# Pooled values of batch 1 on GpSimd, shared casts of q, a later memset and an earlier turn of q in an attention and MoE kernel

## The chip, the cores and the metric

The kernel runs on one core of a Trainium2 chip. The metric is the device time of one execution in microseconds, and the time of the kernel before is the median of three runs.

## The reference

The first stage is an attention whose keys and values are means over groups of eight positions. The second stage is a two-layer network over the attention's output, with g = h - tanh(h) between the layers.

```python
batch, heads, S, D, pool = 8, 8, 576, 64, 8
k_p = k.reshape(B, H, S // pool, pool, D).mean(axis=3)
v_p = v.reshape(B, H, S // pool, pool, D).mean(axis=3)
attn = softmax(q @ k_p.T / sqrt(D))          # 576 x 72 for each head
x = (attn @ v_p).transpose(0, 2, 1, 3).reshape(4608, 512)
h = x @ w_in                                 # 512 x 2048
out = (h - tanh(h)) @ w_out                  # 2048 x 512
```

Inputs and output are float32.

## The kernel before

The kernel takes the 4608 tokens in nine groups of 512 (`NG`). Groups 0 to 7 are the first 512 rows of each batch, and group 8 gathers the last 64 rows of all batches (`xT_last`). TensorE (PE) works through the matmuls in an order written out by hand, and each of the other engines has its own written order too. Nothing is moved by a scheduler: `tc.manual_schedule()` keeps the program's order on each engine, and semaphores between engines follow from the data.

For a batch the work is this. Keys and values come in as float32 (`k_raw`, `v_raw`, two buffers each, so batches 1, 3, 5 share one). `pool_k` adds the eight rows of a group in three steps, four, two and one at a time, and leaves `kd`, two copies of the pooled keys in bf16. PE or the DMA transposes these, and the pieces are put into `KB`. The values are added up in the same way and spread into `VB`, which also carries a column of the constant 8. Queries are cast to bf16 into `q_bf`, turned into `qT` (by `q_pe_transpose` for batches 0 and 1, and by `q_dma_transpose` on the SP queue from batch 2 on). Then follow scores, `exp` on ScalarE into `E`, the product with `VB`, and a division by the last column on VectorE (`x_sb`). The result is transposed into `xT`.

Group 0 of the network uses plain matmuls: `mlp_h_mms` with `mlp_h_act` for the first layer, `mlp_o(g, tb, qd, gts)` for one quarter `qd` of the second layer's sum of the block `tb` of 128 tokens (four matmuls of 512 columns). Between those quarters the attention of batch 1 is interleaved; this is the first stage that the change touches. From group 1 on the second layer is a Strassen-like scheme with seven products (`products`) in place of eight, for which sums and differences of quarters of w_out are prepared (`sum0` to `sum3`, `negated`, in `w2s`). In these groups `h_pair` computes two of the 16 blocks of the first layer into two banks, takes tanh on ScalarE (L647) and the difference on VectorE (L648). The seven pairs of group 1 use the banks 6, 4, 2, 6, 0, 2, 4 in turn. The queries of batch 2 are cast (`q_cast_part`, L196 and L201, ScalarE) and turned (`q_dma_transpose`, L214 and L219, SP) between these pairs; this is the second stage that the change touches. The scores of the next batch (`head_scores`, L446) stand between the halves of the products and use the banks 2 and 3, then 4 and 5.

In the stage of batch 1 the queries come from `q1_bf` and `q1_tail`, which lie in the space of `w2s` until the sums are written there. Two copies at L1017 reorder them into `q_bf`, four heads each, one by VectorE and one by ScalarE. `evac` takes a PSUM tile out to SBUF, by the engine named. PSUM tiles of this stage come in turn from the banks 4, 5, 6, 7: one for the keys, one for their remainder, four for q, one for its tail, then the scores. `pool_v1(ta, tb)` adds the values of batch 1 for the tiles `ta` to `tb` on VectorE (L303) and places them with `v_main` (L323) or, for the remainder, `v_left` (L333). The instruction that it returns is stored as `placed`, and two of GpSimd's `sum3` instructions are made to wait for it.

GpSimd (POOL) builds constants at the start, issues the loads of the weights (`load_w1`, `load_w2`), pools the keys of batch 1 up to the last addition, which VectorE does (L270), issues two more loads of w_out, and pools keys and values of the later batches.

Of the kernel before, what the change touches and what calls it, by code (L numbers as in the profile page):

```python
# [34 lines left out]
NM = 4  # L35
# [8 lines left out]
def kernel(  # L44
# [178 lines left out]
    def q_pe_transpose(b, hps, eng=None):  # L223
        qT, _ = q_tiles(b)
        for hp in hps:
            ps = ps_any([128, QA], FP32, "qT_ps")
            for j in range(R):
                nc.tensor.matmul(
                    ps[:, j * 128 : (j + 1) * 128],
                    lhsT=q_bf[:, j, 2 * hp : 2 * hp + 2, :].rearrange("p h d -> p (h d)"),  # L230
                    rhs=ident[:, :],
                    start=True,
                    stop=True,
                )
            evac(qT[:, :, hp, :], ps.rearrange("p (j c) -> p j c", j=R), eng)
# [61 lines left out]
                out=vps[b][:, :, :], in0=r[:, :, 0, :], in1=r[:, :, 1, :], op=ALU.add  # L297
            )

    def pool_v1(ta, tb):  # L300
        r = v_raw[1].rearrange("p t (j d) -> p t j d", d=D)
        for n in (4, 2, 1):
            nc.vector.tensor_tensor(  # L303
                out=r[:, ta:tb, 0:n, :],
                in0=r[:, ta:tb, 0:n, :],
                in1=r[:, ta:tb, n : 2 * n, :],
                op=ALU.add,
            )
        if ta == NM:
            return v_left(VB[1], r[:, NM, 0:1, :], nc.vector)  # L310
        return v_main(VB[1], r[:, :, 0:1, :], nc.vector, ta, tb)

    vps = {}

# [6 lines left out]
    def v_main(vb, vs, eng, t0, t1):  # L321
        n = t1 - t0
        return eng.tensor_tensor(  # L323
            out=vb[:, 2 * t0 : 2 * t1, 0:D].rearrange("p (t s) d -> p t s d", s=2),
            in0=vs[:, t0:t1, :, :].to_broadcast([128, n, 2, D]),
            in1=mask[:, 2 * t0 : 2 * t1, :]
            .rearrange("p (t s) o -> p t s o", s=2)
            .to_broadcast([128, n, 2, D]),
            op=ALU.mult,
        )  # L330

    def v_left(vb, vs, eng):
        return eng.tensor_tensor(  # L333
            out=vb[:, 2 * NM :, 0:D],
            in0=vs.to_broadcast([128, NM, D]),
            in1=mask[:, 2 * NM :, :].to_broadcast([128, NM, D]),
            op=ALU.mult,
        )
# [21 lines left out]
    def k_transpose(b, alloc, engs=(nc.vector.tensor_copy, nc.scalar.copy)):  # L360
        kd = kdups.pop(b)
        ps = alloc([128, NM, 128], FP32, "kT_ps")
        for t in range(NM):
            turn_tile(ps[:, t, :], kd, t)
        kb_main(KB[b % 2], ps, 0, NM, engs)
        ps = alloc([128, 128], FP32, "kT_ps")
        turn_tile(ps[:, :], kd, NM)
        kb_left(KB[b % 2], ps, nc.vector.tensor_copy)
# [37 lines left out]
    def scores_wide(b, ts):  # L406
        if b not in E_tiles:
            E_tiles[b] = work.tile([128, H, S], BF16, name="E", tag="E", bufs=1)[:, 0:NT, :]
        E = E_tiles[b]
        for t in ts:  # L410
            ps = ps_any([128, QA], FP32, "s_ps")
            score_mms(b, t, ps[:, :], False)
            nc.scalar.activation(out=E[:, t, 0:QA], in_=ps[:, :], func=ACT.Exp, scale=SCALE)
# [196 lines left out]
    def mlp_o(g, tb, qd, gts):  # L610
        if qd == 0:
            o_tiles[tb] = bank((1, 2, 3, 0)[tb], [128, DM])
        o_ps = o_tiles[tb]
        i0 = W2_ORDER[qd]
        for i in range(i0, i0 + 4):
            nc.tensor.matmul(  # L616
                o_ps[:, :],
                lhsT=gts[i][:, tb * 128 : (tb + 1) * 128],
                rhs=w2b[:, i, :],
                start=(i == 0),  # L620
                stop=(i == NHID - 1),
            )
        if qd == 3:
            if tb < 2:
                nc.vector.tensor_copy(out=O[:, tb, :], in_=o_ps[:, :])
            else:
                nc.scalar.copy(out=O[:, tb, :], in_=o_ps[:, :])
            if tb % 2:
                store(g, tb - 1, tb + 1, nc.sync)
# [136 lines left out]
    def load_w2(i, n):  # L766
        w2_dmas.append(
            nc.gpsimd.dma_start(out=w2b[:, i : i + n, :], in_=w2_src[:, i : i + n, :])
        )
# [39 lines left out]

    make_identity(nc, ident)  # L810
    nc.gpsimd.memset(q_bf[64:128, R, :, :], 0.0)
    nc.gpsimd.memset(w2s[64:128, 3, 6:8, :], 0.0)
    nc.gpsimd.memset(mask[:, :, :], 1.0)
    for m, base, step, cm in (
        (mask[:, 0 : 2 * NM : 2, 0], G - 1, 0, -1),
# [27 lines left out]
        out=q1_bf, in_=q[1, :, 0:QA, :].rearrange("h (p j) d -> p h j d", j=R)  # L843
    )
    load_w2(8, 4)
    nc.gpsimd.memset(k_raw[1][:, NM, :], 0.0)
    nc.gpsimd.memset(v_raw[0][:, NM, :], 0.0)
    nc.gpsimd.memset(KB[1][:, :], 0.0)
# [164 lines left out]
    pool_k(1, nc.gpsimd, last=nc.vector)  # L1013
    load_w2(4, 4)
    load_w2(12, 4)
    for h, copy in ((0, nc.vector.tensor_copy), (4, nc.scalar.copy)):
        copy(  # L1017
            out=q_bf[:, 0:R, h : h + 4, :].rearrange("p j h d -> p h j d"),
            in_=q1_bf[:, h : h + 4, :, :],
        )  # L1020
    mlp_o(0, 0, 0, gts)
    mlp_o(0, 1, 0, gts)
    mlp_o(0, 2, 0, gts)
    k_transpose(1, ps_any, (nc.vector.tensor_copy, nc.vector.tensor_copy))
    mlp_o(0, 3, 0, gts)
    q_pe_transpose(1, (0, 1), "act")
    sum1(0)
    pool_v1(0, 2)
    q_pe_transpose(1, (2, 3), "act")
    q_pe_tail(1)  # L1030
    scores_wide(1, (0,))
    placed = pool_v1(2, 4)
    mlp_o(0, 0, 1, gts)
    scores_wide(1, (1,))
    mlp_o(0, 1, 1, gts)
    scores_wide(1, (2, 3))
    scores_ends(1)
    negated(0)
    sum2(0)
# [23 lines left out]
    turn1(3)  # L1063
    av(1, 4, ps_any, True)
    sum0(4)
    for tb in range(4):
        mlp_o(0, tb, 3, gts)
    x_pairs.pop((1, 0))
    x_pairs.pop((1, 1))
    x_dma_transpose(1, 2)  # L1070
    pool_k(2, nc.gpsimd)
    k_dma_transpose(2)
    load_k(3)
    pool_v(2, nc.gpsimd, (0, 1))
    k_place(2, nc.gpsimd.tensor_copy)
# [2 lines left out]
    for g in range(1, NG):  # L1078
        nb = g + 1 if g + 1 < B else None
        nn = g + 2 if g + 2 < B else None  # L1080
        for p in range(NP - 1):
            if g == 1 and 3 <= p < 6:
                q_cast_part(2, p - 3)
                q_dma_transpose(2, p - 3)
            if nb is not None and g > 1 and p < 3:
                q_cast_part(nb, p)
            h_pair(g, p, ((6, 4, 2, 6, 0, 2, 4) if g == 1 else (0, 2, 4, 6, 0, 2, 4))[p], p % 2)
            if g == 1 and p == 1:
                sum2(4)
            if g == 1 and p == 2:  # L1090
                w_sum(b12, b22, b12, ALU.subtract)
            if g == 1 and p == 5:
                load_v(3)
                load_q(3)
                v_spread(2, nc.gpsimd)
            if 3 <= p < 6:
                sum_p(2 * p - 6, 2 * p - 4)
            if g > 1 and p == 0:
                if nb is not None:
                    k_dma_transpose(nb)  # L1100
                store(g - 1, 2, 4, nc.gpsimd)
                store(g - 1, 0, 2, nc.gpsimd)
                if nb is not None:
                    k_place(nb, nc.gpsimd.tensor_copy)
            if nb is not None and g > 1 and p < 3:
                q_dma_transpose(nb, p)
            if nb is not None and g > 1 and p == 2:
                v_spread(nb)
                if nn is not None:
                    load_k(nn)  # L1110
                    load_v(nn)
                    load_q(nn)
        h_one(g, NP - 1, 1, 0, 2)
        h_one(g, NP - 1, 0, 1, 3)
        sum_p(6, 8)
        sum_q(0, 4)
        sum_q(4, 8)
        if nb is not None:
            sum_d(0, 2)
            sum_d(2, 4)  # L1120
        ps_a = Banks(2, 3, 4, 5, 0, 1)
        for u in range(14):
            n, half = u // 2, u % 2
            bk, lhs, rhs = products[n]
            if n == 6 and g == NG - 1:
                break
            product(g, bk, lhs, rhs, 4 * half, 4 * half + 4, n < 2)
            if half:
                after_product(g, n)
            if nb is not None:  # L1130
                if u == 0:
                    head_scores(nb, (0, 1))
                if u == 2:
                    head_scores(nb, (2, 3), True)
                if u in (5, 6, 7, 8, 10):
                    blk = (5, 6, 7, 8, 10).index(u)
                    av(nb, blk, ps_b1, True)
                    if blk in (1, 3, 4):
                        x_dma_transpose(nb, blk // 2)
                if u == 6 and nn is not None:  # L1140
                    pool_k(nn, nc.gpsimd)
                    pool_v(nn, nc.gpsimd)
        if g < NG - 1:
            nc.scalar.copy(out=O[:, 0:2, 0:HD], in_=chain(g, C1))  # L1144
# [37 lines left out]
```

## Time and profile before

| what | value |
|---|---|
| time, median of three runs | 286.15 us (286.08 to 286.72) |
| profiled execution, its own time | 286.49 us |
| profiled execution, span from first to last instruction | 284.7 us |
| granted TensorE clock | 0.997 |
| PE busy | 275.9 us (97% of the span) |
| VectorE (DVE) busy | 224.2 us (79%) |
| ScalarE (ACT) busy | 155.5 us (55%) |
| GpSimd (POOL) busy | 119.1 us (42%) |
| moved by DMA | 49.82 MB, 175 GB/s on average |

The span is that of the profiled execution, and what lies around it is not in the trace. Busy time of an engine is the time in which an instruction of it is under way; an instruction that waits for something inside the engine counts as busy. Start times in the views are microseconds from the start of the span. In the timeline a row is a start, a length, the engine, the line of the kernel, the operation, what is written and read, the number of instructions merged in it, and, in brackets, the engine's idle time before it with what ended it.

### The profile page before, as it was taken

To read this page: it belongs to the slowest core of one execution; us is meant where nothing else is said; L and a number is where in the kernel's file an instruction comes from. 1 tells how busy PE (TensorE), PEld (TensorE's weight loads), DVE (VectorE), ACT (ScalarE), POOL (GpSimd) and SP (SyncE) were. 2 spreads that over 40 slices of the span, in tenths; PEclk is the share of its full clock that TensorE was granted. 3 is DMA by queue.
4 is the path that set the end of the run, shared out by engine and by line. 5 is a ranking of instruction groups with operands and counts; after the bars stand their busy time and mean duration, and the time that the engine had idled before them with its cause. 6 is when DMAs were issued, how large, how long until landed. Compare 5 with 4: busy or idle time off the path is not lost.

```text
span 284.7 us, 5459 instructions
## 1 busy us (share of the span) xinstructions
PE 275.9 (97%) x2156; PEld 180.2 (63%) x2156; DVE 224.2 (79%) x339; ACT 155.5 (55%) x208; POOL 119.1 (42%) x129
## 2 busy tenths in 40 slices
PE   7899999998999999999999999999999999999994
PEld 2454455644894489448954895479547954884583
DVE  5569898789875998599859985998599839936983
ACT  2837676386628672857186718670868056216610
POOL 8810809972299019901990099009910110010000
PEclk9999999999999999999999999999999999999998
DMA  7999999889847894769789986896640540012014
GB/s 245 230 210 279 259 206 305 270 236 229 246 83 144 290 324 83 143 226 350 130 107 270 324 149 124 272 323 131 114 161 0 76 157 0 2 74 77 0 39 111
DMA packets 66731, 49.82 MB, mean 175 GB/s; under 512 B 42088, under 2 KB 55928, under 8 KB 66706
## 3 DMA queue, kind: packets, MB, share of 16 engines
q1 hardware_dynamic: 56082, 34.92, 48.8%
q0 software_dynamic: 8432, 12.72, 18.8%
q10 hardware_dynamic: 2192, 1.84, 2.2%
q8 instruction: 17, 0.28, 0.5%
q14 instruction: 8, 0.07, 0.1%
HBM read 36.70 MB, written 9.44 MB: 162 GB/s over the span
## 4 chain that ended last, share of the span: by engine, by line
PE 90%; DMA 4%; ACT 2%; issue 1%; DVE 1%; ACTq 0%
PE PS L634 36%; PE PS L691 35%; PE PS L588 5%; PE PS L616 5%; PE PS L472 3%; PE PS L446 3%; DMA qT<-q_bf 2%; DMA q_raw<-in_q_dram 2%; PE PS L398 1%; PE PS L781 1%; PE PS L487 1%; ACT q_bf L196 1%; ACT qT L144 1%; PE PS L875 0%; PE PS L936 0%
## 5 line engine op out<-in xcount | busy, mean ns | idle before, releaser
L634 PE MATMUL PS<-xT,w1b 128*128 128x512 bf16 (+1 forms) x504 | 98.0, 355 | 0.0
L648 DVE TENSOR_TENSOR Gt<-PS,TS 128x1024 bf16<-128x1024 f32 x56 | 68.4, 1222 | 33.7 <-ACT TS L647 33.7
L634 PEld LDWEIGHTS <-w1b 128*128 128x128 f16 x576 | 56.3, 98 | 52.8
L647 ACT ACTIVATE TS<-PS 128x1024 f32<-128x1024 f32 x56 | 57.4, 1025 | 29.5 <-PE PS L634 27.4
L735 POOL TENSOR_TENSOR m<-O,m 128x512 f32<-128x512 f32 x6 | 7.6, 1259 | 77.3 <-ACT m L733 77.3
L691 PE MATMUL PS<-w2s,Dg 128*128 128x256 f16 x256 | 30.2, 273 | 0.0
L467 ACT ACTIVATE E<-PS 72x1024 bf16<-72x1024 f32 (+1 forms) x30 | 26.1, 930 | 4.8 <-PE PS L446 4.6
L691 PEld LDWEIGHTS <-Gt 128*128 128x128 bf16 x256 | 23.6, 98 | 6.9 <-issue 2.5
L261 POOL TENSOR_TENSOR k_raw<-k_raw 128x512 f32<-128x512 f32 (+2 forms) x13 | 21.1, 1636 | 14.6 <-DMA k_raw<-in_k_dram 14.6
L691 PEld LDWEIGHTS <-P 128*128 128x128 bf16 x256 | 24.6, 98 | 3.0
L691 PEld LDWEIGHTS <-Dg 128*128 128x128 bf16 x256 | 24.6, 98 | 2.8
L656 DVE TENSOR_TENSOR P<-Gt 128x1024 bf16<-128x1024 bf16 x32 | 22.0, 687 | 0.5
L707 POOL DMA_DIRECT2D out_dram<-O x14 | 7.7, 551 | 31.7 <-DVE O L745 29.5
L742 ACT COPY m<-PS 128x512 f32<-128x512 f32 x8 | 4.7, 586 | 29.6 <-PE PS L691 29.6
L666 DVE TENSOR_TENSOR Dg<-Gt 128x1024 bf16<-128x1024 bf16 x32 | 20.4, 683 | 0.0
L523 DVE TENSOR_TENSOR x_sb<-PS,rden 128x512 bf16<-128x512 f32 x28 | 19.4, 692 | 1.0
L282 POOL TENSOR_TENSOR v_raw<-v_raw 128x512 f32<-128x512 f32 (+1 forms) x12 | 18.2, 1537 | 0.0
L691 PE MATMUL PS<-w2s,Gt 128*128 128x256 f16 x128 | 16.4, 273 | 0.0
L691 PE MATMUL PS<-w2b,P 128*128 128x256 f16 x128 | 16.3, 273 | 0.0
L691 PE MATMUL PS<-w2s,Q 128*128 128x256 f16 x128 | 16.3, 272 | 0.0
L691 PE MATMUL PS<-w2b,Gt 128*128 128x256 f16 x128 | 16.3, 272 | 0.0
L1144 ACT COPY O<-PS 128x512 f32<-128x512 f32 x7 | 4.1, 587 | 21.9 <-PE PS L691 21.9
(125 smaller groups left out, 403.9 us busy)
## 6 DMA issues: line engine op xcount, KB each, us to landing
k_raw<-in_k_dram SPq DMA_DIRECT2D x7, 1024.0 KB, 5.9
out_dram<-O POOLq DMA_DIRECT2D x14, 512.0 KB, 4.3
v_raw<-in_v_dram SPq DMA_DIRECT2D x6, 1024.0 KB, 8.0
q_raw<-in_q_dram SPq DMA_DIRECT2D x6, 1024.0 KB, 10.6
w1b<-in_moe_w_in_dram POOLq DMA_DIRECT2D x4, 512.0 KB, 13.3
w2b<-in_moe_w_out_dram POOLq DMA_DIRECT2D x4, 512.0 KB, 16.6
v_raw<-in_v_dram SPq DMA_DIRECT2D x2, 512.0 KB, 12.5
out_dram<-O SPq DMA_DIRECT2D x2, 512.0 KB, 3.5
```

The costliest lines, as they stand in the source:

```text
L261: eng.tensor_tensor(out=r[:, ta:tb, 0:4, :], in0=r[:, ta:tb, 0:4, :], in1=r[:, ta:tb, 4:8, :], op=ALU.add,)
L282: eng.tensor_tensor(out=r[:, ta:tb, 0:4, :], in0=r[:, ta:tb, 0:4, :], in1=r[:, ta:tb, 4:8, :], op=ALU.add,)
L467: nc.scalar.activation(out=e, in_=ps, func=ACT.Exp, scale=SCALE)
L523: nc.vector.tensor_tensor(out=x_sb[:, :, :, :], in0=ps[:, :, :, 0:D], in1=rden[:, :, :, :].to_broadcast([128, 2, 4, D]), op=ALU.mult,)
L588: nc.tensor.matmul(h_tiles[i][:, :], lhsT=w1b[:, fb, i * 128 : (i + 1) * 128], rhs=xT[g][:, :, fb, :], start=(fb == 0), stop=(fb == NFB - 1),)
L616: nc.tensor.matmul(o_ps[:, :], lhsT=gts[i][:, tb * 128 : (tb + 1) * 128], rhs=w2b[:, i, :], start=(i == 0), stop=(i == NHID - 1),)
L634: nc.tensor.matmul(dst[:, t0 * 128 : t1 * 128], lhsT=w1b[:, fb, i * 128 : (i + 1) * 128], rhs=x[:, t0:t1, fb, :], start=(fb == 0), stop=(f ...
L647: nc.scalar.activation(out=t2, in_=PS[:, b0 : b0 + 2, :], func=ACT.Tanh)
L648: nc.vector.tensor_sub(out=Gt[:, p, :, :], in0=PS[:, b0 : b0 + 2, :], in1=t2)
L656: nc.vector.tensor_tensor(out=P[:, a:b, :], in0=Gt[:, a:b, 0, :], in1=Gt[:, a:b, 1, :], op=ALU.add)
L666: return nc.vector.tensor_tensor(out=Dg[:, a:b, :, :], in0=Gt[:, a:b, :, 0:HT], in1=Gt[:, a:b, :, HT:TG], op=ALU.subtract,)
L691: nc.tensor.matmul(part(g, bk, tt), lhsT=lhs(k, slice(tt * 128, (tt + 1) * 128)), rhs=rhs[:, k, :], start=(first and k == 0 and (tt == 0 o ...
```

## The change

Six edits are in it.

- The three additions for the main tiles of batch 1's values are made by GpSimd, for all four tiles at once, right behind its two last loads of w_out. VectorE places the result in two instructions, later than before. The remainder (`ta == NM`) stays on VectorE.
- Both copies of batch 1's q into `q_bf` are made by VectorE.
- The four PSUM tiles of q of batch 1 are taken out by ScalarE and VectorE in turn, and two of them are turned ahead of the last quarter-0 output block. `sum1(0)` stands behind them, and the four scores stand in twos.
- A memset of part of `w2s` on GpSimd moves behind the first loads.
- The last quarter of group 0's output, with its stores, is written behind the transposes of `x_end` and of batch 2's `kd`, which changes the order on SP.
- The casts and transposes of q of batch 2 begin at pair 2 instead of pair 3 of group 1; the loads of v and q of batch 3 and the spread of batch 2's values follow at pair 4 instead of 5.

```diff
--- before.py
+++ after.py
@@ -297,18 +297,18 @@
                 out=vps[b][:, :, :], in0=r[:, :, 0, :], in1=r[:, :, 1, :], op=ALU.add
             )
 
-    def pool_v1(ta, tb):
+    def pool_v1(ta, tb, eng=nc.vector):
         r = v_raw[1].rearrange("p t (j d) -> p t j d", d=D)
         for n in (4, 2, 1):
-            nc.vector.tensor_tensor(
+            eng.tensor_tensor(
                 out=r[:, ta:tb, 0:n, :],
                 in0=r[:, ta:tb, 0:n, :],
                 in1=r[:, ta:tb, n : 2 * n, :],
                 op=ALU.add,
             )
         if ta == NM:
-            return v_left(VB[1], r[:, NM, 0:1, :], nc.vector)
-        return v_main(VB[1], r[:, :, 0:1, :], nc.vector, ta, tb)
+            v_left(VB[1], r[:, NM, 0:1, :], nc.vector)
+        return r[:, :, 0:1, :]
 
     vps = {}
 
@@ -809,7 +809,6 @@
 
     make_identity(nc, ident)
     nc.gpsimd.memset(q_bf[64:128, R, :, :], 0.0)
-    nc.gpsimd.memset(w2s[64:128, 3, 6:8, :], 0.0)
     nc.gpsimd.memset(mask[:, :, :], 1.0)
     for m, base, step, cm in (
         (mask[:, 0 : 2 * NM : 2, 0], G - 1, 0, -1),
@@ -843,6 +842,7 @@
         out=q1_bf, in_=q[1, :, 0:QA, :].rearrange("h (p j) d -> p h j d", j=R)
     )
     load_w2(8, 4)
+    nc.gpsimd.memset(w2s[64:128, 3, 6:8, :], 0.0)
     nc.gpsimd.memset(k_raw[1][:, NM, :], 0.0)
     nc.gpsimd.memset(v_raw[0][:, NM, :], 0.0)
     nc.gpsimd.memset(KB[1][:, :], 0.0)
@@ -1013,27 +1013,29 @@
     pool_k(1, nc.gpsimd, last=nc.vector)
     load_w2(4, 4)
     load_w2(12, 4)
-    for h, copy in ((0, nc.vector.tensor_copy), (4, nc.scalar.copy)):
-        copy(
+    for h in (0, 4):
+        nc.vector.tensor_copy(
             out=q_bf[:, 0:R, h : h + 4, :].rearrange("p j h d -> p h j d"),
             in_=q1_bf[:, h : h + 4, :, :],
         )
+    vs = pool_v1(0, NM, nc.gpsimd)
     mlp_o(0, 0, 0, gts)
     mlp_o(0, 1, 0, gts)
     mlp_o(0, 2, 0, gts)
     k_transpose(1, ps_any, (nc.vector.tensor_copy, nc.vector.tensor_copy))
+    q_pe_transpose(1, (0,), "act")
+    q_pe_transpose(1, (1,), "dve")
     mlp_o(0, 3, 0, gts)
-    q_pe_transpose(1, (0, 1), "act")
+    q_pe_transpose(1, (2,), "act")
+    q_pe_transpose(1, (3,), "dve")
+    q_pe_tail(1)
+    v_main(VB[1], vs, nc.vector, 0, 2)
+    placed = v_main(VB[1], vs, nc.vector, 2, 4)
     sum1(0)
-    pool_v1(0, 2)
-    q_pe_transpose(1, (2, 3), "act")
-    q_pe_tail(1)
-    scores_wide(1, (0,))
-    placed = pool_v1(2, 4)
+    scores_wide(1, (0, 1))
     mlp_o(0, 0, 1, gts)
-    scores_wide(1, (1,))
+    scores_wide(1, (2, 3))
     mlp_o(0, 1, 1, gts)
-    scores_wide(1, (2, 3))
     scores_ends(1)
     negated(0)
     sum2(0)
@@ -1063,13 +1065,13 @@
     turn1(3)
     av(1, 4, ps_any, True)
     sum0(4)
-    for tb in range(4):
-        mlp_o(0, tb, 3, gts)
     x_pairs.pop((1, 0))
     x_pairs.pop((1, 1))
     x_dma_transpose(1, 2)
     pool_k(2, nc.gpsimd)
     k_dma_transpose(2)
+    for tb in range(4):
+        mlp_o(0, tb, 3, gts)
     load_k(3)
     pool_v(2, nc.gpsimd, (0, 1))
     k_place(2, nc.gpsimd.tensor_copy)
@@ -1079,9 +1081,9 @@
         nb = g + 1 if g + 1 < B else None
         nn = g + 2 if g + 2 < B else None
         for p in range(NP - 1):
-            if g == 1 and 3 <= p < 6:
-                q_cast_part(2, p - 3)
-                q_dma_transpose(2, p - 3)
+            if g == 1 and 2 <= p < 5:
+                q_cast_part(2, p - 2)
+                q_dma_transpose(2, p - 2)
             if nb is not None and g > 1 and p < 3:
                 q_cast_part(nb, p)
             h_pair(g, p, ((6, 4, 2, 6, 0, 2, 4) if g == 1 else (0, 2, 4, 6, 0, 2, 4))[p], p % 2)
@@ -1089,7 +1091,7 @@
                 sum2(4)
             if g == 1 and p == 2:
                 w_sum(b12, b22, b12, ALU.subtract)
-            if g == 1 and p == 5:
+            if g == 1 and p == 4:
                 load_v(3)
                 load_q(3)
                 v_spread(2, nc.gpsimd)
```

## The prediction

> **What bounds the kernel now.** I start from the first part of the page, engine totals.
>
> ```profile
> PE 275.9 (97%) x2156; PEld 180.2 (63%) x2156; DVE 224.2 (79%) x339; ACT 155.5 (55%) x208; POOL 119.1 (42%) x129
> ```
>
> TensorE runs 97% of the 284.7 us span, so a change pays only where it fills a TensorE gap and costs only where it opens one. The stages tell how much there is to fill: in the windows 34.00 to 54.30 us and 54.30 to 70.00 us (the two that the change touches) PE is busy 19.93 of 20.30 us and 14.85 of 15.70 us. So at most 0.37 and 0.85 us can be won. The waits of PE, and the one long wait of POOL, up to 86 us name these gaps (columns: total, times, longest):
>
> ```profile
> PE PS L446 <- DMA qT<-q_bf: 0.8, 1, 0.8
> PE PS L398 <- ACT qT L144: 0.2, 1, 0.2
> ...
> POOL w2s L674 <- DVE VB L323: 7.2, 1, 7.2
> ```
>
> The first is in the chain that ended last, which leaves PE for ScalarE's casts of q of batch 2 and their transpose by DMA:
>
> ```profile
> 62.43 1.05 ACT q_bf L196
> 63.48 0.03 ACT TS L647
> 63.51 6.34 DMA qT<-q_bf
> 69.84 0.14 issue
> 69.98 0.62 PE PS L446 x4
> ```
>
> The third says that GpSimd is free from 35.46 to 42.70 us. The change puts batch 1's value pooling there. What VectorE does in that gap is in the timeline (start, length, engine, line):
>
> ```profile
> 33.94 1.52 POOL L768 DMA_DIRECT2D w2b<-in_moe_w_out_dram  x2
> ...
> 35.62 0.82 DVE L270 TENSOR_TENSOR kd<-k_raw 128x640 bf16<-128x640 f32 x1
> ...
> 36.60 0.43 DVE L1017 COPY q_bf<-w2s 128x1024 bf16<-128x1024 bf16 x1 [0.17 <-DMA w2s<-in_q_dram]
> 37.19 0.45 DVE L342 CAST KB<-PS 64x288 bf16<-64x288 f32 x1 [0.16 <-PE PS L352]
> ...
> 39.46 0.38 PE L398 MATMUL PS<-qT,KB 128*128 128x512 bf16 x1 [0.21 <-ACT qT L144]
> ```
>
> kd, the first copy of q and the casts of KB lie on the path to the first score of batch 1 at 39.46. PE has just enough matmuls to cover them.
>
> **What the skill says.** The Trainium skill, SBUF — State Buffer, section Who interferes with whom: VectorE and GpSimd share one port pair as an exclusive lock for a whole instruction; a VectorE operation with two SBUF inputs contends with a GpSimd operation that reads SBUF, and so does a copy in a two-port mode. The trace agrees on the first, at two places:
>
> ```profile
> 80.91 1.54 POOL L267 TENSOR_TENSOR k_raw<-k_raw 128x640 f32<-128x640 f32 x1
> 81.06 1.93 DVE L743 TENSOR_TENSOR m<-m,m 128x512 f32<-128x512 f32 x1 [0.46 <-ACT m L742]
> ...
> 48.24 3.03 POOL L261 TENSOR_TENSOR k_raw<-k_raw 128x512 f32<-128x512 f32 x2 [0.24 <-DMA k_raw<-in_k_dram]
> 49.52 2.30 DVE L674 TENSOR_TENSOR w2s<-w2b 128x1024 f16<-128x1024 f16 x1
> 51.35 1.87 POOL L267 TENSOR_TENSOR k_raw<-k_raw 128x640 f32<-128x640 f32 x1
> ```
>
> L743 ends at 82.99, 0.55 us after GpSimd's instruction (80.91 + 1.54 = 82.45); L674 (0.69 elsewhere) ends at 51.82, 0.55 after 51.27. The waiter goes first when the lock comes free: GpSimd's next, L267, is 0.33 longer than the 1.54 it takes alone. The engines so alternate, and a waiter saves some 0.14 us of start-up (0.69 - 0.55). VectorE operations with one input in PSUM (L601, L523: 0.69) are not lengthened beside GpSimd. For the copy: VectorE: DVE Perf Modes, The perf-mode tier table, gives bf16 SBUF copies four elements a cycle, through both ports. L1017's 0.43 us for 1,024 elements fits that (plain speed would be over 1 us); no such copy beside GpSimd's work is in this trace.
>
> **The change part by part.**
>
> *Values of batch 1.* VectorE loses six L303 instructions, 2 x (0.68 + 0.43 + 0.29) = 2.80 us, none on PE's path. GpSimd gets three with 1024, 512 and 256 elements a partition. Its rows L261 and L267 give 1.27 (512), 1.54 (640), 2.90 us (1280), a straight line: 2.35, 1.27, 0.72. They stand right behind the two L768 issues, so the first starts at 33.94 + 1.52 = 35.46; both halves of v, issued at 19.60 and 21.22, land 12.5 us later, by 33.7. That is 0.16 us before kd starts (35.62). By the lock, with 0.14 off for each waiter:
> - GpSimd's first ends 35.46 + 2.35 = 37.81; kd 37.81 + 0.68 = 38.49 (was 36.43);
> - second: 38.49 + 1.13 = 39.62; first q copy: 39.62 + 0.29 = 39.91 (was 37.03);
> - third: 39.91 + 0.58 = 40.49; second q copy: 40.49 + 0.29 = 40.78.
>
> Behind these in VectorE's order are the three KB casts (1.00 us from start to end before; 0.97 with the overlap): 41.75. Then its cast of the second q pair (0.60, the pace of L625's copies of the same 128x512 f32): 42.35. The first score of batch 1 reuses that bank, so PE goes on at about 42.41 instead of 39.46: **+2.95 us**. PE's other work fits in: keys turned at 38.6, the first two q pairs at 40.0, one output block until 41.3, the other two pairs when KB's casts have left the banks. If VectorE's kd came first, the same alternation gives 0.3 less. GpSimd may itself start up to 0.52 earlier (next item). I take **+2.7**, bounds 2.2 to 3.3.
>
> *The memset* (L812, 0.52 us) goes behind the first loads, so the load of v, the four of w1 and the first of w2 start up to 0.52 us sooner (what follows waits for L840's data at 10.58, as before). No PE wait names w1b or w2b, so nothing is gained; the early loads share the DMA engines with q and k, which PE's first wait (1.2 us at L228) depends on. Bounds -0.1 to +0.2; I take +0.05.
>
> *The q copies and casts.* ScalarE loses one copy (1.05) and two casts (0.51 each) in a stage where it is busy 11.81 of 20.30 us; VectorE gets 0.43 and 2 x 0.60. This alone would free the 0.2 us wait at L398, counted in the rival below. sum1(0) (0.69) and both value placements (0.43 each) move behind the casts and end by 44.5, ahead of their readers. GpSimd's four L674 wait for the placements as before.
>
> *The order of outputs.* On SP the transposes of x_end and kd now stand before two output stores (0.36 + 1.15 us of issue); keys of batch 2 are turned and placed sooner. The four loads of v and q of batch 3 and GpSimd's three spread DMAs go one pair (1.73 us) sooner, behind their transposes; their readers come a stage later. Costed at nothing.
>
> *q of batch 2 one pair sooner.* The first cast follows the second tanh at 58.96 instead of 60.58, so the second ends near 62.1, not 63.5, and its transpose lands near 68.4 (same 6.34 us). PE wants it at 69.13 (69.98 - 0.85): this wait goes. What is late next: the second pair of these scores reuses the banks of h_pair 6, whose VectorE subtraction (L648 at 68.33, 1.22 us) ends at 69.55. VectorE runs without a gap from 60.7, and ScalarE's third tanh now ends at 61.02 (behind the cast), not 60.69, so that subtraction ends near 69.9; PE waits for it instead of 69.44. I take a gain of **0.45**, bounds 0.1 to 0.85.
>
> Sum: +2.7 + 0.05 - 0.45 = +2.3. Against the profiled execution's 286.49 us (span 284.7 and 1.8 around it) 288.8; it stands 0.34 above the median of the runs, so against 286.15 I forecast 288.4.
>
> **The rivals.**
>
> *The copy does not need the lock* (no run of before shows it). Only kd is late: 38.49, copies end 39.1, KB's casts 40.1, q's cast 40.7, first score near 40.8: +1.3, sum +0.9: **287.05**. Against it: the copy's rate and the skill's page.
>
> *No collision, so faster.* If GpSimd's pooling does not meet kd and the copies, for instance because its start slips behind both and VectorE's casts (from PSUM) run free, the 0.2 us at L398 and 0.45 at L446 are won, up to 0.37 and 0.85 if every gap closes: -0.6, **285.55**, at best 285.0. It decides from the point where GpSimd's first addition starts later than 37.1, that is 1.6 us later than the issues leave it. For it: GpSimd's 7.2 us of idleness. Against: it starts when its own queue says, and nothing there waits.
>
> *The change does not do what it says:* batch 2's q transposes land no sooner, since the DMA engines or SP hold them (share 0.85 in that stage). Then the 0.45 is missing: 288.9.
>
> **How the numbers follow.** Collision with kd and copies 0.73, of which 0.1 with batch 2's wait left; collision with kd alone 0.13; none 0.12; something else 0.02. The likeliest gives 288.4. Its own bounds reach from +1.5 to +3.3 (286.15 + 3.3 = 289.4); the range goes down to 286.6, the low end of the second case, and leaves out the third and the tails. About 0.3% (0.86 us) is what a measurement can tell from no change. Faster by more than that takes nearly all gaps closed: 0.09; within it, the rest of the third case and half of the second: 0.13; slower 0.78.
>
> **What would show it.** Right: GpSimd's first L303 at 35 to 35.5; kd over 2 us long; the L1017 copies 1 to 2 us each; the waits of PE at L352, L228 and L398 behind DVE adding to some 2.7 us between 36.9 and 43; the wait at L446 named after DVE's Gt, under 0.6. Wrong: copies of 0.43 us while L303 runs, the first score before 40, a kd of 0.82, or L446 still waiting 0.8 for the DMA.

## The result, and the profile after

The change makes the kernel slower. Its median is 290.1 us (289.39 to 291.42, four runs) against 286.12 us (285.45 to 286.72, four runs) before: ratio 1.0145 with a 95% interval of 1.010 to 1.019. The forecast was 288.4 us with a range to 289.4, so the direction was right and the size too small. The profiled execution took 291.42 us (span 289.4); it is the slowest of the four, and its granted TensorE clock is 0.985. The other three had 0.990, 0.999 and 1.000 at 290.48, 289.39 and 289.71 us.

The engine totals and the row of the granted clock, from the page of the kernel after (a digit is a fortieth of the span; 9 is full speed):

```profile
PE 278.2 (96%) x2156; PEld 181.3 (63%) x2156; DVE 228.0 (79%) x336; ACT 153.8 (53%) x205; POOL 123.9 (43%) x132
...
PEclk9999968999999999999999999999999999999998
```

PE is busy 2.3 us longer for the same 2156 matmuls. No work was added, so some of them ran slower; the row says where: slices six and seven, 36 to 51 us. PE's waits up to 90 us (total, times, longest):

```profile
PE PS L352 <- DVE kd L270: 3.2, 2, 2.5
...
PE PS L228 <- DVE q_bf L1017: 0.7, 1, 0.7
PE PS L446 <- DVE Gt L648: 0.3, 1, 0.3
```

Two new waits are there, for kd and for the copy of q. The wait for the DMA of q is gone, and 0.3 us behind VectorE's subtraction stands in its place. The timeline of the collision:

```profile
34.18 1.53 POOL L768 DMA_DIRECT2D w2b<-in_moe_w_out_dram  x2
34.97 3.80 DVE L270 TENSOR_TENSOR kd<-k_raw 128x640 bf16<-128x640 f32 x1
35.72 5.04 POOL L303 TENSOR_TENSOR v_raw<-v_raw 128x1024 f32<-128x1024 f32 x3
38.69 2.35 DVE L1017 COPY q_bf<-w2s 128x1024 bf16<-128x1024 bf16 x2
38.83 0.71 PE L352 MATMUL PS<-ident,kd 128*128 128x128 bf16 x5 [2.54 <-DVE kd L270]
40.23 1.03 PE L228 MATMUL PS<-ident,q_bf 128*128 128x128 bf16 x8 [0.69 <-DVE q_bf L1017]
41.06 1.91 PE L616 MATMUL PS<-w2b,Gt 128*128 128x512 f16 x4
43.85 1.04 PE L398 MATMUL PS<-qT,KB 128*128 128x512 bf16 x2
```

kd takes 3.80 us (0.82 before), the two copies 2.35 us (0.43 for one before). PE stands still for 2.54 us, and then four matmuls of 512 columns (L616) take 1.91 us, against 1.03 in the kernel before:

```profile
37.05 1.03 PE L616 MATMUL PS<-w2b,Gt 128*128 128x512 f16 x4
```

The first score of batch 1 starts at 43.85, 4.39 us later than before. At the second set of batch 2's scores (L446) PE is 4.70 us late (77.09 against 72.39), and the span is longer by just that: nothing after them adds or gives back. The executions of the kernel after have 2.01 to 2.09 us outside their span, though, where the profiled one of the kernel before has 1.8; this second difference is taken up below.

### The profile page after: what moved, and what is told of

Its sections match the earlier page's. It is cut to its first block, busy times and chain, and to the rows that moved or that the text cites. A ratio compares the mean times of both kernels' runs of the same rounds, so it can differ in the third digit from the quotient of the medians.

```text
span 289.4 us, 5458 instructions
## 1 busy us (share of the span) xinstructions
PE 278.2 (96%) x2156; PEld 181.3 (63%) x2156; DVE 228.0 (79%) x336; ACT 153.8 (53%) x205; POOL 123.9 (43%) x132
## 4 chain that ended last, share of the span: by engine, by line
PE 87%; DVE 6%; DMA 2%; ACT 2%; issue 1%; SPq 0%; ACTq 0%
PE PS L634 35%; PE PS L691 34%; PE PS L588 5%; PE PS L616 4%; PE PS L472 3%; PE PS L446 3%; DMA k_raw<-in_k_dram 2%; DVE Gt L648 2%; DVE kd L270 1%; PE PS L398 1%; PE PS L487 1%; PE PS L228 1%; DVE P L656 1%; ACT TS L647 1%; DVE q_bf L1017 0%
## 5 line engine op out<-in xcount | busy, mean ns | idle before, releaser
L691 PE MATMUL PS<-w2s,Dg 128*128 128x256 f16 x256 | 30.2, 272 | 0.0
L691 PEld LDWEIGHTS <-Gt 128*128 128x128 bf16 x256 | 23.5, 98 | 6.8 <-issue 2.3
L691 PEld LDWEIGHTS <-P 128*128 128x128 bf16 x256 | 24.6, 98 | 3.0
L691 PEld LDWEIGHTS <-Dg 128*128 128x128 bf16 x256 | 24.6, 98 | 2.8
L616 PE MATMUL PS<-w2b,Gt 128*128 128x512 f16 x64 | 16.7, 401 | 0.0
L691 PE MATMUL PS<-w2s,Gt 128*128 128x256 f16 x128 | 16.4, 273 | 0.0
L691 PE MATMUL PS<-w2b,P 128*128 128x256 f16 x128 | 16.3, 273 | 0.0
L691 PE MATMUL PS<-w2b,Gt 128*128 128x256 f16 x128 | 16.3, 272 | 0.0
L691 PE MATMUL PS<-w2s,Q 128*128 128x256 f16 x128 | 16.3, 272 | 0.0
```

The costliest lines, as they stand in the source:

```text
L616: nc.tensor.matmul(o_ps[:, :], lhsT=gts[i][:, tb * 128 : (tb + 1) * 128], rhs=w2b[:, i, :], start=(i == 0), stop=(i == NHID - 1),)
L691: nc.tensor.matmul(part(g, bk, tt), lhsT=lhs(k, slice(tt * 128, (tt + 1) * 128)), rhs=rhs[:, k, :], start=(first and k == 0 and (tt == 0 o ...
```

## The experiments

The theory on record before the first of these runs was that the values on GpSimd are the whole loss, by the lock. Its rivals were a loss in the other parts, and that GpSimd's additions cost nothing where they stand. The kernel before was timed again beside these runs: its medians are 286.19 us beside the first four, 286.27 beside the next four, and 286.37 beside the last four. The ratios are those of the record, with their 95% intervals; they differ by up to 0.002 from the quotient of two medians.

**Values back on VectorE, the rest of the change kept.**

```diff
-    vs = pool_v1(0, NM, nc.gpsimd)
     ...
     q_pe_tail(1)
+    vs = pool_v1(0, NM)
     v_main(VB[1], vs, nc.vector, 0, 2)
```

> The changed kernel with the additions of batch 1's values back on VectorE, behind its casts of q; the rest of the change is kept. Theory (GpSimd's additions hold the lock that kd and the q copies need): kd falls from 3.80 us to about 0.82, the copies to 0.43 each, the first score of batch 1 comes near 39, PE's clock stays at 0.997, and the time is 285.0 to 285.8 us. Rival (the copy and casts of q that were given to VectorE stand in front of the casts of KB and make PE late): those are still there, so the time stays above 288.

Measured: 288.94 us, ratio 1.0112 [1.0077, 1.0147]. From its timeline and PE's waits:

```profile
35.07 0.81 DVE L270 TENSOR_TENSOR kd<-k_raw 128x640 bf16<-128x640 f32 x1
36.59 0.76 DVE L1017 COPY q_bf<-w2s 128x1024 bf16<-128x1024 bf16 x2 [0.70 <-DMA w2s<-in_q_dram]
```

```profile
PE PS L446 <- DMA qT<-q_bf: 1.7, 1, 1.7
PE PS L566 <- DVE x_sb L523: 1.6, 1, 1.6
```

The collision is gone (kd 0.81, two copies 0.76, first score at 39.03), yet the kernel stays slow. Two waits that the kernel after doesn't have hold PE: 1.6 us for x_sb of batch 1, and 1.7 us for the transposed q of batch 2. The theory of a single loss falls. The rival's number (above 288) came true, but hardly its reason: the first score comes at 39.03, against 39.46 in the kernel before and 38.5 to 39.1 in the variants below that keep its copies and casts. VectorE's copies and casts of q can make PE late by some 0.5 us there, not by 2.7.

**Only the values on GpSimd**, in the kernel before:

```diff
+    vs = pool_v1(0, NM, nc.gpsimd)
     mlp_o(0, 0, 0, gts)
     ...
-    pool_v1(0, 2)
+    v_main(VB[1], vs, nc.vector, 0, 2)
     ...
-    placed = pool_v1(2, 4)
+    placed = v_main(VB[1], vs, nc.vector, 2, 4)
```

> The kernel before with only the additions of batch 1's values given to GpSimd, at the place where the change has them; copies, casts, memset and the turn of q as before. Theory of the lock: kd takes over 3 us, the one q copy on VectorE over 1 us, PE stands still some 2 us at the keys of batch 1, and the time is 288 to 290. Rival (VectorE's casts and copy): the time is within 0.5 of the kernel before, since VectorE has less to do.

Measured: 289.31 us, ratio 1.0120 [1.0098, 1.0142], as the lock would have it.

```profile
34.89 4.04 DVE L270 TENSOR_TENSOR kd<-k_raw 128x640 bf16<-128x640 f32 x1
38.99 0.45 PE L352 MATMUL PS<-ident,kd 128*128 128x128 bf16 x5 [2.79 <-DVE kd L270]
```

So the collision alone costs about 3.1 us, or 2.7 in the two executions whose clock is 1.000 (288.89 and 288.95 us). What the two other losses cost is hidden behind it in the kernel after.

**GpSimd waits for the second copy**, the rest of the change kept:

```diff
     for h in (0, 4):
-        nc.vector.tensor_copy(
+        copied = nc.vector.tensor_copy(
     ...
-    vs = pool_v1(0, NM, nc.gpsimd)
+    vs = pool_v1(0, NM, nc.gpsimd, copied)   # its first addition waits for copied
```

> The changed kernel, with the first of GpSimd's three additions made to wait for VectorE's second copy of q. Theory of the lock: kd takes 0.82, the copies 0.43, GpSimd adds from about 37 to 41.4 while VectorE casts from PSUM, whose lengths stay as they were; the values are placed ahead of their use; the time is 284.9 to 285.8. If issuing the two loads of w_out (1.5 us of GpSimd) holds the lock too, kd still takes 1.3 or more and the time is some 0.5 higher. Rival (VectorE's order): above 288.

Measured: 288.07 us, ratio 1.0074 [1.0050, 1.0098]; the expected gain was missed. From its timeline (in this kernel and those made from it, lines past 320 stand two lines lower: L676 is L674, L325 is L323, L568 is L566, L448 is L446):

```profile
37.13 4.49 POOL L303 TENSOR_TENSOR v_raw<-v_raw 128x1024 f32<-128x1024 f32 x3 [1.41 <-DVE q_bf L1019]
41.65 0.76 DVE L325 TENSOR_TENSOR VB<-v_raw,mask 128x256 bf16<-128x256 f32 x2 [2.08 <-POOL v_raw L303]
42.33 3.81 DVE L676 TENSOR_TENSOR w2s<-w2b 128x1024 f16<-128x1024 f16 x3
42.49 4.65 POOL L676 TENSOR_TENSOR w2s<-w2b 128x512 f16<-128x512 f16 x3 [0.88 <-DVE VB L325]
47.04 0.40 PE L568 MATMUL PS<-ident,x_sb 128*128 128x128 bf16 x4 [1.34 <-DVE x_sb L525]
```

kd takes 0.81 us and the copies 0.76. The additions run beside VectorE's casts from PSUM and disturb nobody. The next collision is in the lines L676. In the kernel before, `sum1(0)` is long done (at 38.22) when GpSimd's sums begin, and only `sum2(0)` and `sum0(0)` meet them:

```profile
42.52 2.25 DVE L674 TENSOR_TENSOR w2s<-w2b 128x1024 f16<-128x1024 f16 x2
42.70 5.31 POOL L674 TENSOR_TENSOR w2s<-w2b 128x512 f16<-128x512 f16 x4 [7.24 <-DVE VB L323]
```

The change moved `sum1(0)` behind the placement, which here waits 2.08 us for GpSimd's additions, so that three VectorE sums stand in that moment. The engines alternate: the first sum takes 0.69 us, the two behind it 1.65 and 1.64, all three 3.81. The division into x_sb behind them is late, and PE waits 1.3 us for it. (With the values back on VectorE the three sums take 3.80 us.) Then PE waits 2.1 us for batch 2's q.

**PE kept busy** by eleven throwaway matmuls in the stall, in the kernel after:

```diff
+    warm_pe(11, b0=7)
     k_transpose(1, ps_any, (nc.vector.tensor_copy, nc.vector.tensor_copy))
```

> The changed kernel with eleven matmuls of zeros in front of the turn of batch 1's keys, which fill PE's standstill there; nothing reads them. In the trace of the changed kernel PE's work from 38.8 to about 45 us ran at half speed after a standstill of 2.5 us. Theory that this slow stretch comes from the standstill and is a part of the loss of its own: kd and the copies are as late as in the changed kernel, PE's matmuls keep 0.216 us each, the clock is 0.997 or more, and the time is 288.8 to 289.5. If the slow stretch has another cause: the clock again at 0.985 to 0.99 and the time 290 or more.

Measured: 289.32 us (289.25 to 289.37, four runs), ratio 1.0114 [1.0099, 1.0129]. The clock is 0.999 to 1.000 in the runs, against 0.985 to 1.000 without the filling.

```profile
35.25 3.38 DVE L270 TENSOR_TENSOR kd<-k_raw 128x640 bf16<-128x640 f32 x1
40.10 0.62 PE L228 MATMUL PS<-ident,q_bf 128*128 128x128 bf16 x8 [0.88 <-DVE q_bf L1017]
42.59 0.59 PE L398 MATMUL PS<-qT,KB 128*128 128x512 bf16 x2
```

kd is as late as ever, but the eight transposes of q take 0.62 us (1.03 without the filling) and the first score starts at 42.59. So the slow matmuls come from PE's standstill. They cost from nothing to 2.1 us from run to run (289.39 to 291.42 against 289.32), some 0.8 us of the median.

**The memset alone**, in the kernel before:

```diff
-    nc.gpsimd.memset(w2s[64:128, 3, 6:8, :], 0.0)      # ahead of the loads
...
     load_w2(8, 4)
+    nc.gpsimd.memset(w2s[64:128, 3, 6:8, :], 0.0)
```

> The kernel before with only the memset of w2s moved behind the first loads. In all traces with the moved memset PE reaches the keys of batch 1 some 0.4 to 0.7 us sooner, and its wait at L228 for the cast of q of batch 0 is 0.4 to 0.7 instead of 1.5 us. If the memset is the cause: 285.4 to 285.8, and L228 waits about 0.7. If it is only how the first loads fall from run to run: within 0.2 of the kernel before.

Measured: 286.18 us, ratio 0.9993 [0.9982, 1.0003]: no difference. PE's waits for q of batch 0 at L228 fall to 0.3 us in all (1.5 before), and waits for data that come no sooner stand in their place:

```profile
PE PS L352 <- DVE kd L270: 0.6, 1, 0.6
PE PS L616 <- DMA w2b<-in_moe_w_out_dram: 0.4, 1, 0.4
```

Nor is the memset the cause of the shorter wait at L228. Kernels that leave it in its place show the same: 0.4 us with only the values on GpSimd, 0.5 and 0.3 us in the two runs that follow. The wait of 1.5 us in the profile of the kernel before is how the first loads fell in that execution.

**The turn of q with its order of outputs**, and then **the turn alone**, each in the kernel before. The second kernel leaves the loop of stores where it was; only the marked lines differ between the two.

```diff
-    for tb in range(4):                # only in the first of the two
-        mlp_o(0, tb, 3, gts)           # only in the first
     ...
     k_dma_transpose(2)
+    for tb in range(4):                # only in the first
+        mlp_o(0, tb, 3, gts)           # only in the first
     load_k(3)
     ...
-            if g == 1 and 3 <= p < 6:
-                q_cast_part(2, p - 3)
-                q_dma_transpose(2, p - 3)
+            if g == 1 and 2 <= p < 5:
+                q_cast_part(2, p - 2)
+                q_dma_transpose(2, p - 2)
     ...
-            if g == 1 and p == 5:
+            if g == 1 and p == 4:
```

> The kernel before with only the later output stores (behind the transposes of x_end and kd on SP) and q of batch 2 turned one pair sooner. Theory of the stores: 1 MB of output and 1.1 MB of keys now go out right ahead of the transposes of q, which take 8 to 9 us to land instead of 5.5 to 6.3; PE's wait for them at L446 is 1 to 2 us instead of 0.8, and the time is 286.4 to 287.4. Rival (as predicted: the sooner cast lands sooner): the wait is under 0.5 and the time 285.4 to 285.9.

> The kernel before with only q of batch 2 turned one pair sooner, and the stores left ahead of the transposes. Theory of the stores: without them in the way the transposes land in about 6 us, PE's wait for the DMA at L446 goes down to under 0.4 or turns into one for VectorE's subtraction of pair 6, and the time is 285.5 to 286.0. If the sooner turn itself brings the transposes into heavier traffic: the wait stays at 0.8 or more and the time at 286.2 or more.

Measured: 289.09 us, ratio 1.0089 [1.0058, 1.0120] with the stores later, and 286.69 us, ratio 1.0017 [1.0006, 1.0028] with the stores kept. The first is slower than either expectation for it; in the second the wait stays, as the last sentence of its expectation has it. SP's queue and the first of the scores, from the timeline of the first and then of the second:

```profile
56.14 1.01 SPq L707 DMA_DIRECT2D out_dram<-O  x2
57.21 0.86 SPq L150 DMA_DIRECT2D k_raw<-in_k_dram  x1
...
59.57 6.42 SPq L214 DMA_TRANSPOSE qT<-q_bf  x2
...
72.00 0.77 PE L446 MATMUL PS<-qT,KB 64*72 64x512 bf16 x4 [3.21 <-DMA qT<-q_bf]
```

```profile
60.35 5.95 SPq L214 DMA_TRANSPOSE qT<-q_bf  x2
...
70.24 0.62 PE L446 MATMUL PS<-qT,KB 64*72 64x512 bf16 x4 [1.29 <-DMA qT<-q_bf]
```

The last pair of heads is issued near 61.7 in both, and the scores start at 72.00 and 70.24. So the two stores (512 KB each), moved from ahead of the transposes of x_end and kd to right ahead of the keys' loads and of q, make PE go on 1.8 us later. In the first kernel PE then also runs slow behind its 3.2 us of waiting (two groups of L691 took 1.89 and 1.71 us, 1.05 and 1.04 before), which is another 1.5 us. And the second kernel answers the question of the prediction: before, the last pair was issued at 63.5 and PE went on at 69.98; with the casts one pair sooner it went on at 70.24. The transposes took 8.4 us to land where they had taken 6.3. A sooner cast brings nothing here.

**All three places mended**: GpSimd waits for the second copy, `sum1(0)` stands ahead of the placement, and the stores ahead of the transposes.

```diff
+    sum1(0)
     v_main(VB[1], vs, nc.vector, 0, 2)
     placed = v_main(VB[1], vs, nc.vector, 2, 4)
-    sum1(0)
     ...
     sum0(4)
+    for tb in range(4):
+        mlp_o(0, tb, 3, gts)
     ...
     k_dma_transpose(2)
-    for tb in range(4):
-        mlp_o(0, tb, 3, gts)
```

> The changed kernel with three of its places mended together: GpSimd's additions wait for the second q copy, sum1(0) stands ahead of the placement of the values, and the output stores stand ahead of the transposes as before. If the loss is made of these three (the lock at kd, three sums against GpSimd's four ahead of x_sb, the stores ahead of the transposes of q), each gone: first score near 39, PE's wait at L566 under 0.4, at L446 under 0.5, time 285.0 to 285.8. If any has another cause it shows as its wait again: 1.3 us at L566 or 2 us at L446, and 286.5 or more.

Measured: 286.79 us, ratio 1.0009 [1.0000, 1.0019]. PE's waits:

```profile
PE PS L448 <- DMA qT<-q_bf: 1.1, 1, 1.1
PE PS L354 <- DVE kd L270: 0.6, 1, 0.6
...
PE PS L568 <- DVE x_sb L525: 0.3, 1, 0.3
```

From 1.0145 to 1.0009: together the three places hold nearly all of the loss. The expected gain over the kernel before isn't there: q still comes at 70.16.

**The order of the sums alone**, in the kernel whose GpSimd waits for the copies; the edit is the upper half of the diff above.

> The changed kernel with GpSimd's additions behind the second q copy and sum1(0) ahead of the placement of the values; the output stores stay behind the transposes. Theory that each loss has its own place: PE's wait at L566 (x_sb) falls from 1.3 to about 0.3 us, the wait at L446 for the transposes of q stays at 2 to 3 us, the time is 287.0 to 288.3. If the stores did not matter: 286.3 or less. If the order of the sums did not matter: L566 still waits 1.3.

Measured: 289.69 us (287.72 to 291.99, four runs), ratio 1.0128 [1.0085, 1.0170]. PE waits 0.3 us for x_sb (1.3 without the edit), and the scores of batch 2 start at 70.83, 1.5 us sooner than the 72.33 without it. The time doesn't follow: behind the wait for q, 1.9 us here, PE runs slow.

```profile
71.47 1.89 PE L693 MATMUL PS<-w2s,Gt 128*128 128x256 f16 x8
73.15 1.78 PE L693 MATMUL PS<-w2b,P 128*128 128x256 f16 x8
```

These two take 1.58 us more than their 1.05 and 1.04 in the kernel before, so what the sums win is lost here. The run with the clock at 0.999 took 287.72 us. The order of the sums was not tried with the stores in their old place and the late sums kept, so its own cost in time is open.

**The loads of batch 3's keys behind q**, in the kernel before, then with q one pair sooner, then in the mended kernel. Here the question was whether these loads hold q up, and whether a version faster than before could be had.

```diff
     k_dma_transpose(2)
-    load_k(3)
     ...
+                load_k(3)              # behind q's transposes
                 load_v(3)
```

> The kernel before with one edit: the load of batch 3's keys (1.1 MB) is issued behind the three transposes of q of batch 2 instead of ahead of them; the casts of q stay where they are. Theory that traffic and not the cast sets when q lands: the transposes take 4 to 5 us instead of 5.5 to 6.3, PE's wait at L446 falls from 0.8 to under 0.2 us (0.3 if VectorE's subtraction is next), time 285.3 to 286.0. Rival (the cast sets it): the wait stays at 0.8 and the time at 286.2.

> The same with q of batch 2 also cast and turned one pair sooner. Theory of the traffic: with the keys out of the way the sooner cast lands sooner too (near 66.5 instead of 69.9 us), the DMA is no longer what L446 waits for; VectorE's subtraction of pair 6 is, for some 0.3 us; time 285.4 to 286.0, no better than the run without the sooner cast. Rival (the sooner cast brings its own gain): 0.3 or more below that run.

> The changed kernel with its three places mended (GpSimd's additions behind the second q copy, sum1(0) ahead of the placement, the output stores ahead of the transposes) and the keys of batch 3 loaded behind the transposes of q. If the parts of the change that are left (values on GpSimd, casts of q shared, the memset later) are worth anything beyond the keys' place, the time is 0.2 us or more below that of the kernel before with the keys' place alone; else the two are equal. I expect 285.4 to 286.1 and no difference.

Measured: 286.28 us, ratio 1.0002 [0.9989, 1.0015]; 286.29 us, 0.9999 [0.9987, 1.0011]; 286.26 us, 1.0005 [0.9994, 1.0016]. From the first one's timeline:

```profile
61.44 3.09 SPq L214 DMA_TRANSPOSE qT<-q_bf  x2
...
68.85 0.41 PE L446 MATMUL PS<-qT,KB 64*72 64x512 bf16 x2
69.58 0.41 PE L446 MATMUL PS<-qT,KB 64*72 64x512 bf16 x2 [0.32 <-DVE Gt L648]
```

With the casts where they were, the scores now start at 68.85, not 69.98. Only 0.2 us of that is an earlier start of this execution (the casts begin at 60.37, not 60.58). So the traffic ahead of the transposes set q's arrival, and not the cast. But VectorE's subtraction is next (0.32 us), and none of the three times can be told from the kernel before. What is left of the change in the third kernel is worth nothing that these runs can show.

## Why the prediction was wrong in size

The forecast is 1.7 us too low (+2.3 against +4.0). In round numbers 0.8 us of that are slow matmuls behind the stall, 0.3 us lie outside the span, and 0.6 us are in the span with the clock kept up.

**The lock chain was right.** Its terms against the trace of the kernel after:

| end of | predicted | measured |
|---|---|---|
| GpSimd's first addition | 37.81 | 38.08 |
| kd | 38.49 | 38.77 |
| first copy of q | 39.91 | 40.17 |
| second copy of q | 40.78 | 41.03 |
| casts of KB | 41.75 | 41.95 |
| cast of the second q pair | 42.35 | 42.67 |

All are within 0.32 us, and the first, 0.27 us, is GpSimd's later start (35.72, not 35.46). The waiter ended 0.69 us after the lock came free for kd and 0.28 for the second copy, where 0.68 and 0.29 were worked out. One part of the fit is luck. The prediction gave GpSimd the lock because its addition would start ahead of kd, and otherwise took 0.3 us off; in the trace kd's row starts 0.75 us ahead of GpSimd's, and kd loses all the same. The rival in which copies need no lock is refuted: two took 2.35 us here, and 0.76 with the additions elsewhere. With the clock kept up the first score starts at 42.59, against 42.41 in the prediction.

**The step that failed first is "PE's other work fits in".** The sum has PE's transposes and the output block at full speed behind a stall that it made itself. They ran at about half speed until about 45 us, and the first score came at 43.85. The Trainium skill, TensorE: Matmul & The Clock Gate, Part 1: The HAM clock gate, says that TensorE's clock is halved after an idle window of about 3.4 us, that the window runs freely, and that the count of slow matmuls differs from run to run. The traces agree on roughly half speed (1.91 against 1.03 us) and on the spread, but not on the length: PE ran slow behind stalls of 2.54, 3.21 and 1.94 us, all shorter than the page's 3.4, and at full clock in the executions with 2.79 and 2.12 us. No length here tells which it will be. This term is 0 to 2.1 us, some 0.8 us of the median.

**"1.8 around it" did not stay.** The sum takes the time outside the span as the same before and after. It is 1.66 to 1.85 us in every execution of the kernel before and of the kernels with these additions on VectorE, and 1.99 to 2.18 us in every execution with them on GpSimd. Moving them back alone brings 2.05 to 1.75 us (medians), and moving only them to GpSimd brings 1.76 to 2.03. So the values on GpSimd cost some 0.3 us that no view of the trace shows. Why is open.

**The choice of +2.7 was too low.** With the clock kept up the span is 287.3 us, 2.9 us longer than the 284.4 at the median of the kernel before beside it (2.6 longer than the profiled 284.7), against the sum of 2.3. I had taken 2.7 us, not the 2.95 that was worked out, for an earlier start of GpSimd, and it started 0.26 us later. What is left of the 0.6 us is not separated.

**The memset was right as nothing.** In the kernel after PE reached the keys some 0.5 us sooner (36.29 against 36.77), which the memset does not explain, as shown above. kd did not end sooner, so the stall only began earlier.

**The 0.45 us of the sooner turn do not exist as predicted.** The wait at L446 did go, with Gt's 0.3 us in its place as forecast, but a late PE is enough for that: PE comes to it 5 us later, and with only the values on GpSimd, q's turn left in its place, the wait for the DMA is gone as well (0.5 us for Gt instead). The turn alone measures 1.0017. The assumption that failed is "same 6.34 us" from issue to landing, 8.4 us there; the rival that the DMA engines hold q was right on this part.

**"The order of outputs", "costed at nothing", failed, hidden.** The stores right ahead of q bring the turn from 1.0017 to 1.0089. In the kernel after, PE's lateness covers them.

**"End by 44.5, ahead of their readers" looked at the wrong readers.** In the kernel whose GpSimd waits for the copies the placements and `sum1(0)` do end early, by 43.02. But `sum2(0)` and `sum0(0)` stand behind them and meet GpSimd's sums one place later: they end at 46.14, not 44.77, and x_sb with them is late. The line of GpSimd's four L674 stood in the prediction, without the same lock applied to it. In the kernel after this loss is hidden too.

**The rival "no collision, so faster" was wrong.** Its condition, GpSimd's first addition later than 37.1, was made (37.13), and the kernel took 288.07 us, not 285.55: the two hidden losses stood next, and the 0.3 us outside the span.

## What to carry to other kernels

When a step moves work onto a lock, apply the lock to everything that the move brings side by side, the later sums too, and ask what each edit costs once the largest loss is gone: losses that hide behind one another don't add up (3.1 us alone, 2.8 us for the turn with its stores, 4.0 us together). Compare the time as well as the span: what a move costs can lie where no view shows it (0.3 us here). A stall of 2 to 3 us on TensorE should be given a second term, for slow matmuls behind it, with its spread. Before a producer is moved sooner to end a wait for a DMA, look at what stands ahead of that DMA on its queue: here the last pair was issued 1.8 us sooner and came no sooner.

## What the runs showed of the hardware

- kd began before GpSimd's shown start of L303 and still lost the lock: 0.75 us before it in the kernel after, 0.97 us with the values alone, 0.31 us with PE filled. With no addition queued behind the DMA issues (34.60 to 36.12) kd took 0.81 us right through them. So a queued addition holds VectorE up sooner than its row shows, and the issue of DMAs alone does not. Why is open; a row of GpSimd may also start late in the trace.
- The two transposes of q landed 5.5 and 6.3 us after their issue in the kernel before, 7.0 and 8.4 us with the turn one pair sooner, and 8.1 and 10.1 us with the stores right ahead of the keys' loads and of them as well. With the keys' loads (1.1 MB) behind them no landing is in the trace; the second was issued at 63.30, and PE began the scores at 68.85 without a wait for it, so it took at most 5.6 us.
- Three additions moved from VectorE to GpSimd lengthen the time outside the span from 1.75 to 2.05 us.
